# A linear attention followed by a two-layer perceptron on one core: rows of w, u and g spread by matmul, more transposes by DMA, and a new order

## The chip, the cores and the metric

The kernel runs on one core of a Trainium2 chip. The metric is the time on the device in microseconds (us) of one execution. The core has five engines that take their instructions each in its own order and wait for one another by semaphores: TensorE (PE in the profile; PEld is its loading of weights), VectorE (DVE), ScalarE (ACT), GpSimd (POOL) and SyncE (SP), which here only issues DMAs. ACT and POOL can issue DMAs too. All queues share 16 DMA engines.

## What is computed

Inputs r, k and v have 4 batches, 8 heads, 768 steps and 48 channels a head; w and u have one value for each head and channel. For each batch and head a 48 x 48 state is carried over the steps:

```
cur   = outer(u * k_t, v_t)
y_t   = r_t @ (state + cur)
state = w[:, None] * state + outer(k_t, v_t)
```

The heads are joined to rows x of 384 values (4 x 768 rows). Then each row goes through a LayerNorm and a perceptron with a residual:

```
xn  = (x - mean(x)) / sqrt(var(x) + 1e-6) * g
out = x + relu(xn @ w_ch1) @ w_ch2        # 384 -> 1536 -> 384
```

All inputs and the output are fp32.

## The kernel before, in words

The steps are cut into 24 chunks of 128 (chunk i is steps 128*(i % 6) onward of batch i // 6). In a chunk the recurrence is turned into matmuls: with Fr = w^t and Fk = w^(-t-1), scaled rows r*Fr and k*Fk make a score matrix, which is masked to the strictly lower part; the state of the chunks before enters by one more product, and the term with u is a factor per head and step (cc) times v. For each chunk there are these steps, with the names that the order uses:

- LK, LR, LV load k, r and v (192 KB each, in runs of 192 B). SK and SR scale k and r and write them as bf16 to sc. CV makes v bf16.
- TR transposes sc on PE, eight 128 x 128 blocks, and TC copies the result from PSUM to trs. From some chunk on TD does both at once, a DMA transpose from sc to trs.
- Q multiplies the two halves of trs. AT makes the scores on PE, and AM masks them into A (DVE).
- S makes on PE the factors cc (by uwI, which holds u*w) and the chunk's addition to the state; CC copies cc out. ZU and ZD form the next state Z with WLZ = w^128.
- VB forms Vb = v*cc. Y makes on PE the state's and the scores' part of the result, and X (DVE) adds Vb, writes a row tile x and sums it up.

For each of the 24 row tiles the perceptron then has: SQ (ACT, the sum of squares), XN (subtract the mean and multiply by g, to xn in bf16), LT and XT (three transposes on PE and a copy to xT) or LTD (one DMA transpose for a whole group), UP (PE, hp = w1 times xT, a PSUM tile of 512 columns), RL (ReLU to hT, on ACT or DVE), DN (PE, four of the twelve blocks of the second matmul at a time), RS (POOL, the inverse deviation), OT (DVE, o*rs + x) and STO (store). Tiles go in groups: 0 to 7 alone, 8 to 19 in pairs, 20 to 23 alone. UP,16g+m is part m of group g, of three for a group of one tile and six for a pair; DN,4i+d is part d of tile i. The last tile is split into two halves of columns (DA, DB, OA, OB, SA, SB).

Nothing schedules this at run time. The string PLAN lists every step with its index and its engine ("v" DVE, "s" ACT, "g" POOL; a DMA with "-" is issued by SP, with "s" by ACT; PE steps have "-" as well), and each engine takes its instructions in the order of that list. Each kind of buffer is a ring of a given number (8 for k and r, 10 for v, 6 for sc and trs, 3 for xn, 4 for xT, 4 for hT). DU steps are dummy matmuls of so many columns, put into PE's order where it would otherwise be idle.

Ahead of the first chunk, w is loaded spread over 128 partitions (WB, from ACT's queue). ACT takes its logarithm (LN) and makes Fr and Fk (FR, FK: exponentials scaled by the partition's number). w and u are also loaded turned, a channel to a partition (ROWS, four DMAs of single values, L186); from these POOL makes uwI (UW) and ACT makes WLZ (WL). g is loaded spread as well (GB, L181). The weights come by six DMAs issued by POOL (IW1 and IW2, 384 KB each, L256 and L259), of which part n of w_ch1 and part n of w_ch2 are tiles of their own. MP clears the padding of sc, MI and MM make the identity and the mask.

Lines that the prediction speaks of: TR L284, AT L320, AM L330, S L351 to L364, Y L393 and L401, X L408, SQ L415, XN L421 and L422, RS L428 and L431, LTD L435, TD L305, LT L443, UP L458, RL L474 (ACT) and L476 (DVE), DN L486, OT L542, copies L163 (ACT) and L165 (DVE, POOL), products L168, loads L262 (k), L265 (r), L268 (v).

Of the kernel before, what the change touches and what calls it, by code (L numbers as in the profile page):

```python
# [7 lines left out]
FP32 = mybir.dt.float32  # L8
# [9 lines left out]
WB,0,s LK,0,- MP,2,v MI,0,g MP,1,v TL,0,s LR,4,- MP,5,v MP,3,v LR,0,- MW,0,v MP,0,v ROWS,3,- LN,0,s ROWS,1,- FR,0,s LR,1,- FK,0,s ROWS,2,- SK,0,v  # L18
LK,2,- LK,1,- SR,0,v ROWS,0,- MZ,0,v LV,0,- DU,7984,- TR,0,- MP,4,v LR,2,- TC,0,s SR,4,g LV,1,- MM,0,g DU,2848,- AT,0,- LK,3,- Q,0,g AM,0,v LK,4,-
LR,6,- CV,0,s SK,1,v LR,3,- UW,0,g WL,0,s SR,1,v LV,2,- DU,4720,- S,0,- SK,2,v Y,0,- GB,0,- TR,1,- ZU,0,v CC,0,s VB,0,g CV,1,s LK,6,- SR,2,v  # L20
TC,1,s LR,5,- SK,3,v LK,5,- Q,1,v DU,2704,- TR,2,- X,0,v LV,3,- S,1,- TC,2,s SK,4,v AT,1,- LV,4,- AM,1,v CC,1,s DU,1056,- TR,4,- LR,7,- SR,3,g
VB,1,v TC,4,s DU,448,- Y,1,- AT,2,- LK,7,- IW1,0,g X,1,v CV,2,s DU,224,- TR,3,- LV,5,- SR,6,v Q,2,g ZU,1,v TC,3,s LV,6,- AM,2,v SK,6,g DU,1712,-
S,2,- SQ,1,s LR,9,- XN,0,v IW1,1,g DU,656,- Y,2,- LV,7,- Q,4,v SK,5,g LT,0,- AT,3,- SR,5,v XT,0,v CC,2,v AM,3,v DU,1104,- TR,6,- Q,3,g TC,6,s
ZU,2,v VB,2,g DU,1216,- AT,4,- XN,1,v LR,8,- DU,592,- TR,5,- CV,3,s IW1,2,g X,2,v UP,0,- IW2,0,g AM,4,v TC,5,s S,3,- RL,0,s LT,1,- CC,3,v ZU,3,v
AT,5,- VB,3,g XT,1,s XN,2,v Y,3,- Q,5,g UP,17,- LR,10,- CV,4,s X,3,v SQ,2,s UP,1,- XN,3,v RL,17,s S,4,- RL,1,v LT,3,- UP,16,- XT,3,s ZU,4,v
SQ,3,s LK,8,- Y,4,- CC,4,v SR,7,g AM,5,v LT,2,- RL,16,s S,5,- UP,48,- IW2,1,g XT,2,s UP,18,- CC,5,s RL,48,s IW2,2,g AT,6,- RL,18,v UP,34,- RS,2,g
VB,4,v Q,6,g UP,32,- RL,34,s LK,9,- DN,0,- RL,32,v SK,7,g UP,50,- X,4,v LK,10,- UP,49,- RS,3,g AM,6,v RL,50,s TR,7,- CV,5,g RL,49,s UP,2,- XN,4,v
SQ,4,s UP,33,- TC,7,v RL,2,s RS,4,g Y,5,- Q,7,v RL,33,s LT,4,- VB,5,g AT,7,- SQ,0,s XT,4,v LV,10,- DN,1,- RS,0,g X,5,v UP,65,- XN,5,v DN,2,-
LV,8,- CV,6,v SR,9,g UP,64,- OT,0,v LT,5,- LV,9,- Y,6,- RL,64,v S,6,- RS,1,g DN,4,- AM,7,v CC,6,s RL,65,s LK,14,- SR,8,g DN,5,- XT,5,s CV,7,s
# [33 lines left out]
def kernel(  # L63
# [526 lines left out]
```

## Time and profile before

| | us |
|---|---|
| median of 3 runs (lowest to highest) | 162.78 (160.44 to 163.22) |
| the profiled execution | 160.98 |
| its span, first to last instruction | 159.2 |
| PE busy | 143.0 (90%) |
| DVE busy | 132.3 (83%) |
| POOL busy | 88.3 (55%) |
| ACT busy | 69.4 (44%) |
| DMA, mean rate | 167 GB/s |

Busy time is the time in which an engine has some instruction under way. Matmuls overlap one another, so a busy PE isn't yet PE at its best rate; the dummy matmuls count as busy too. "DMA share" in a stretch is the sum of what packets took on the 16 DMA engines, divided by 16 times the stretch; packets overlap, so it can pass 1. In a group of instructions (line, engine, operation, output<-inputs, shape, count) the two numbers behind the bar are the busy time in us and the mean of one in ns; behind the next bar stands the idle time of the engine ahead of them and what ended it. In the timeline a bracket holds the idle time before an instruction and what released it.

### The profile page before, as it was taken

Reading aid. Unit: us, or ns where it says so; the run is one execution under the profiler, and the core shown is the slowest. Engines: PE = TensorE matmul, PEld = TensorE weight load, DVE = VectorE, ACT = ScalarE, POOL = GpSimd, SP = SyncE. Lnnn points to the kernel's source line nnn. Section 1 sums busy time; section 2 is a strip of 40 time slices with the busy share of each in tenths; the row PEclk is TensorE's granted clock in tenths of the full one; section 3 lists DMA queues with packets and bytes.
Section 4 is the critical chain, followed back from the end, with each engine's and each line's share of the span. In section 5 each row is a group of like instructions: output and inputs, shape, how many; then the busy total and the mean of one; then the engine's idle time right before and its main releaser. Section 6 shows DMA issues by size and latency. Waiting matters only on the chain.

```text
span 159.2 us, 4407 instructions
## 1 busy us (share of the span) xinstructions
PE 143.0 (90%) x1769; PEld 109.1 (69%) x1769; DVE 132.3 (83%) x265; ACT 69.4 (44%) x155; POOL 88.3 (55%) x119
## 2 busy tenths in 40 slices
PE   5896959499999989799999988997999999999991
PEld 2244737398877777677787757784787767888881
DVE  2457998696899999998889999999979999996132
ACT  3427644653821844646653644614184412700510
POOL 2332465899594665979769865559327420850100
PEclk9999999999999999999999999999999999999999
DMA  3899999999989959999999999895899772314212
GB/s 89 156 173 211 184 184 191 216 199 232 198 157 182 192 110 215 168 218 122 247 235 183 219 224 145 207 214 105 180 215 197 157 195 45 124 29 124 99 54 101
DMA packets 100356, 26.64 MB, mean 167 GB/s; under 512 B 95344, under 2 KB 99952, under 8 KB 100336
## 3 DMA queue, kind: packets, MB, share of 16 engines
q1 hardware_dynamic: 98560, 23.80, 75.0%
q0 software_dynamic: 1632, 2.36, 8.9%
q8 instruction: 14, 0.23, 0.6%
q10 hardware_dynamic: 144, 0.20, 0.5%
q14 instruction: 6, 0.05, 0.1%
HBM read 19.27 MB, written 4.72 MB: 151 GB/s over the span
## 4 chain that ended last, share of the span: by engine, by line
DVE 37%; PE 29%; SPq 10%; POOL 8%; issue 8%; DMA 6%; ACT 0%; DVEq 0%; POOLq 0%
PE hp L458 13%; PE o L486 12%; DVE A L330 8%; DVE xn L422 6%; DVE x L408 4%; SPq L265 4%; DVE Z L168 3%; DMA kf<-in_k_dram 3%; DVE ot L542 3%; DVE hT L476 3%; DVE ZS L377 3%; POOL sc L168 3%; DVE sc L168 3%; DMA trs<-sc 2%; SPq L262 2%
## 5 line engine op out<-in xcount | busy, mean ns | idle before, releaser
L458 PE MATMUL hp<-xT,w_sb 128*128 128x128 bf16 (+1 forms) x648 | 57.6, 238 | 0.6 <-DVE hT L476 0.6
L486 PE MATMUL o<-w_sb,hT 128*128 128x384 bf16 x276 | 53.3, 326 | 2.9 <-DVE ot L542 2.9
L458 PEld LDWEIGHTS <-w_sb 128*128 128x128 bf16 x648 | 48.7, 114 | 5.2 <-issue 0.7
L474 ACT ACTIVATE hT<-hp 128x512 bf16<-128x512 f32 x51 | 30.2, 596 | 44.9 <-PE hp L458 44.3
L486 PEld LDWEIGHTS <-hT 128*128 128x128 bf16 x276 | 25.2, 97 | 15.5 <-issue 3.4
L330 DVE TENSOR_TENSOR A<-at,mask 128x1024 bf16<-128x1024 f32 x24 | 29.1, 1215 | 1.8 <-PE at L320 1.8
L383 POOL TENSOR_TENSOR Vb<-vf,cc 128x384 f32<-128x384 f32 x14 | 12.3, 876 | 13.7 <-DVE cc L165 7.0
L422 DVE SCALAR_TENSOR_TENSOR xn<-x,mu,g_bc 128x384 bf16<-128x384 f32 x24 | 19.0, 792 | 0.8
L168 POOL TENSOR_TENSOR sc<-rf,Fr 128x384 bf16<-128x384 f32 x14 | 15.6, 1117 | 7.2 <-DMA rf<-in_r_dram 7.2
L542 DVE SCALAR_TENSOR_TENSOR ot<-o,rs,x 128x384 f32<-128x384 f32 x23 | 14.0, 610 | 5.8 <-PE o L486 5.7
L168 POOL TENSOR_TENSOR q<-trs 128x512 bf16<-128x512 bf16 x13 | 16.3, 1251 | 2.3 <-ACT trs L163 2.2
L428 POOL TENSOR_SCALAR rs<-sq 128x1 f32<-128x1 f32 (+1 forms) x18 | 3.9, 217 | 23.5 <-ACT sqj L415 22.5
L168 POOL TENSOR_TENSOR sc<-kf,Fk 128x384 bf16<-128x384 f32 x12 | 13.4, 1119 | 5.8 <-DMA kf<-in_k_dram 5.8
L476 DVE TENSOR_SCALAR hT<-hp 128x512 bf16<-128x512 f32 x21 | 14.3, 683 | 2.6 <-PE hp L458 2.6
L408 DVE SCALAR_TENSOR_TENSOR x<-y,Vb 128x384 f32<-128x384 f32 x24 | 13.2, 550 | 2.8 <-POOL Vb L383 2.1
L415 ACT ACTIVATE sqj<-x,sm 128x384 bf16<-128x384 f32 x24 | 14.7, 613 | 1.8 <-DVE cc L165 1.1
L227 PE MATMUL o<-warm 128*128 128x512 bf16 x45 | 13.3, 433 | 1.7 <-DVE u_p L194 1.7
L163 ACT COPY trs<-tr 128x1024 bf16<-128x1024 bf16 x8 | 8.1, 1011 | 12.5 <-PE tr L284 12.5
L168 DVE TENSOR_TENSOR sc<-kf,Fk 128x384 bf16<-128x384 f32 x12 | 9.0, 750 | 5.0 <-ACT Fk L235 4.5
L431 POOL TENSOR_TENSOR rs<-rs,expo 128x1 f32<-128x1 f32 (+1 forms) x18 | 12.0, 668 | 1.5
L320 PE MATMUL at<-trs 48*128 48x128 bf16 x192 | 9.6, 219 | 1.8 <-DVE A L330 1.7
L163 ACT CAST vv<-vf 128x384 bf16<-128x384 f32 x16 | 8.1, 513 | 4.5 <-DMA vf<-in_v_dram 4.5
(66 smaller groups left out, 169.8 us busy)
## 6 DMA issues: line engine op xcount, KB each, us to landing
kf<-in_k_dram SPq DMA_DIRECT2D x24, 192.0 KB, 4.3
rf<-in_r_dram SPq DMA_DIRECT2D x24, 192.0 KB, 4.4
vf<-in_v_dram SPq DMA_DIRECT2D x24, 192.0 KB, 4.2
out_dram<-ot SPq DMA_DIRECT2D x23, 192.0 KB, 2.3
w_sb<-in_moe_w_ch_dram POOLq DMA_DIRECT2D x6, 384.0 KB, 5.9
trs<-sc SPq DMA_TRANSPOSE x15, 3.6
w_bc<-in_w_dram ACTq DMA_DIRECT2D x1, 192.0 KB, 3.8
g_bc<-in_moe_g_ln_dram SPq DMA_DIRECT2D x1, 192.0 KB, 5.7
```

The lines of the kernel that those rows point to most:

```text
L163: nc.scalar.copy(out=out, in_=in_)
L168: engines[e].tensor_tensor(out=out, in0=in0, in1=in1, op=ALU.mult)
L227: nc.tensor.matmul(out=warm_ps[0][:], lhsT=warm[:, :P], rhs=warm[:], start=True, stop=True)
L330: nc.vector.tensor_tensor(out=AA(i)[:, a:b].rearrange("p e q t -> p (e q) t"), in0=psum["at", i][:, a:b].rearrange("p e q t -> p (e q) t") ...
L408: nc.vector.scalar_tensor_tensor(out=xx(i)[:], in0=psum["y", i][:, :C], scalar=1.0, in1=Vb(i)[:], op0=ALU.mult, op1=ALU.add, accum_out=sm[ ...
L415: nc.scalar.activation(out=sqj[:], in_=xx(i)[:], func=ACT.Square, bias=sm[i][:], scale=-float(C), accum_out=sq[g][:, j : j + 1])
L422: nc.vector.scalar_tensor_tensor(out=xn(g)[:, j], in0=xx(i)[:], scalar=mu[i][:], in1=g_bc[:], op0=ALU.subtract, op1=ALU.mult,)
L458: nc.tensor.matmul(out=t[:, a * gw : (a + 1) * gw], lhsT=w1_sb[n][:, kc, fb::FB], rhs=xT(g)[:, :size, kc, :], start=(kc == 0), stop=(kc == ...
L474: nc.scalar.activation(out=o, in_=s, func=ACT.Relu)
L476: nc.vector.tensor_relu(out=o, in_=s)
L486: nc.tensor.matmul(out=psum["o", i][:, :C], lhsT=hT(g)[:, fk, j * P : (j + 1) * P], rhs=w2_sb[d][:, a, :], start=(fk == 0), stop=(fk == FK ...
L542: nc.vector.scalar_tensor_tensor(out=ot(i)[:], in0=psum["o", i][:, :C], scalar=rs[g][:, j : j + 1], in1=xx(i)[:], op0=ALU.mult, op1=ALU.add,)
```

## The change

w, u and g are each loaded as a single row on one partition (WF by SP; UF and GF by ACT). LN works on that row. A matmul with a column of ones (WBM, one partition deep, fp32) spreads the row of logarithms to 128 partitions in PSUM, from where FR and FK read it. GBM spreads g in the same way, and GB is now DVE's copy out of PSUM. UWR (POOL) makes u*w on the row, and WT turns the rows of logarithms and of u*w into columns by eight matmuls with one column of ones each; UW (DVE, two copies) and WL (ACT) read these. The spread DMAs WB and GB and the four ROWS are gone, and so is a logarithm in WL. MO is a step of DVE with three small memsets.

XN may also be POOL's: there it is the mean, a subtraction to a new tile xc, and a product. MP may be POOL's.

DMA transposes of k and r begin with chunk 8 (before: 9), those of the LayerNorm rows with tile 8, group 8 (before: tile 16, group 12): 16 TD and 10 LTD instead of 15 and 6, 8 TR and 8 LT instead of 9 and 16. The list of steps is a new one throughout, with other engines for many steps. By count (before, after): XN on POOL 0, 6; SK on POOL 12, 16; SR on POOL 14, 11; CV on POOL 6, 11, on ACT 16, 7, on DVE 2, 6; VB on POOL 14, 15; ZD on POOL 6, 7; RL on DVE 21, 15; XT on ACT 12, 5, on DVE 4, 3; TC on ACT 8, 6, on DVE 1, 2; MP on POOL 0, 4. Q stays at 13 on POOL. Dummy columns: 25,264 before, 15,664 after.

```diff
 PLAN = """
-WB,0,s LK,0,- MP,2,v MI,0,g MP,1,v TL,0,s LR,4,- MP,5,v MP,3,v LR,0,- MW,0,v MP,0,v ROWS,3,- LN,0,s ROWS,1,- FR,0,s LR,1,- FK,0,s ROWS,2,- SK,0,v
-LK,2,- LK,1,- SR,0,v ROWS,0,- MZ,0,v LV,0,- DU,7984,- TR,0,- MP,4,v LR,2,- TC,0,s SR,4,g LV,1,- MM,0,g DU,2848,- AT,0,- LK,3,- Q,0,g AM,0,v LK,4,-
...
+MW,0,v UF,0,s LK,0,- MP,3,v MP,1,g MO,0,v GF,0,s WF,0,- LR,1,- TL,0,s LR,0,- LV,0,- LN,0,s UWR,0,g DU,2992,- WBM,0,- LR,4,- MP,2,g MI,0,g LK,1,-
+MP,0,g MP,4,g GBM,0,- MM,0,g FK,0,s LK,2,- FR,0,s SK,0,g WT,0,- SR,1,v LV,1,- SR,0,v MZ,0,v LR,2,- DU,432,- TR,0,- WL,0,s SK,1,g TC,0,v LV,3,-
+Q,0,v DU,2208,- TR,1,- LV,2,- GB,0,v CV,0,v TC,1,s DU,464,- AT,0,- CV,1,v LK,3,- SK,2,v UW,0,v Q,1,g AM,0,v DU,1632,- S,0,- LK,5,- CV,3,g SR,2,v
+LR,3,- DU,1120,- Y,0,- AT,1,- ZU,0,v TR,2,- CC,0,v LK,4,- AM,1,v VB,0,g S,1,- TC,2,s LR,5,- IW1,2,g X,0,v CV,2,g ZU,1,v DU,1968,- Y,1,- SQ,0,s
+LV,4,- Q,2,v AT,2,- IW1,1,g CC,1,v SR,3,v DU,272,- S,2,- VB,1,g SK,3,v AM,2,v CC,2,s DU,240,- TR,3,- TC,3,s X,1,v LK,6,- XN,0,v Q,3,g XN,1,v
+DU,3616,- LT,0,- AT,3,- XT,0,s ZU,2,v IW1,0,g AM,3,v DU,720,- UP,2,- SK,4,g LT,1,- Y,2,- RL,2,s MP,5,v XT,1,v SR,4,g S,3,- LR,6,- UP,18,- ZU,3,v
...
+DN,25,- CV,11,s X,9,v UP,112,- XN,9,v LR,14,- DN,26,- AM,10,v RL,112,s RS,7,g LTD,8,- UP,114,- SR,13,g S,10,- OT,6,v UP,113,- LK,14,- SK,11,v ZD,9,g AT,12,-
+SR,11,g RL,113,s DN,28,- TD,11,- SQ,9,s ZU,10,v SR,14,g DN,29,- SK,13,v RL,114,s AM,12,v Y,10,- SQ,8,s STO,3,- UP,129,- CC,10,s TD,13,- VB,10,g UP,133,- ZD,10,v
...
+RL,240,s UP,242,- X,23,v DN,84,- RL,242,s XN,23,v UP,256,- SQ,22,s LTD,17,- DN,85,- RL,256,v UP,257,- UP,258,- RL,257,s DN,86,- SQ,23,s UP,272,- RL,258,s RS,17,g OT,21,v
+UP,273,- RS,16,g STO,21,- DN,88,- RL,273,s DN,89,- RL,272,s DN,90,- UP,274,- OT,22,v DB,0,- RL,274,s STO,22,- DA,0,- DA,1,- STO,20,- DA,2,- DB,1,- OA,23,v DB,2,-
+SA,23,- OB,23,v SB,23,-
 """
...
-    w_bc = const.tile([P, C], FP32, name="w_bc")
+    w_row = const.tile([1, H, D], FP32, name="w_row")
+    u_row = const.tile([1, H, D], FP32, name="u_row")
+    g_row = const.tile([1, C], FP32, name="g_row")
+    ones = const.tile([1, P], FP32, name="ones")
+    ln_row = const.tile([1, H, DP], FP32, name="ln_row")
+    uw_row = const.tile([1, H, DP], FP32, name="uw_row")
...
-    def WB(i, e):
-        queues[e].dma_start(out=w_bc[:], in_=spread(w))
-
-    def GB(i, e):
-        queues[e].dma_start(out=g_bc[:], in_=spread(moe_g_ln))
...
+    def row(t):
+        return bass.AP(tensor=t.tensor, offset=t.offset, ap=[[C, 1], [1, C]])
+
+    def WF(i, e):
+        queues[e].dma_start(out=w_row[:].rearrange("p h d -> p (h d)"), in_=row(w))
...
     def LN(i, e):
-        nc.scalar.activation(out=ln_bc[:].rearrange("p h d -> p (h d)"), in_=w_bc[:], func=ACT.Ln)
+        nc.scalar.activation(out=ln_row[:, :, :D], in_=w_row[:], func=ACT.Ln)
+
+    def WBM(i, e):
+        t = psum["wb"] = ps.tile([P, 512], FP32, name="y")
+        nc.tensor.matmul(out=t[:, :C], lhsT=ones[:], rhs=ln_row[:, :, :D], start=True, stop=True)
+        psum["ln"] = t[:, :C].rearrange("p (h d) -> p h d", h=H)
...
+    def GB(i, e):
+        copy(e, g_bc[:], psum["gb"][:, 0].rearrange("p q t -> p (q t)")[:, :C])
+
+    def UWR(i, e):
+        times("g", uw_row[:, :, :D], u_row[:], w_row[:])
+
+    def WT(i, e):
+        t = psum["wt"] = ps.tile([P, 512], FP32, name="s")
+        first = True
+        for a, src in enumerate((ln_row, uw_row)):
+            flat = src[:].rearrange("p (q e) d -> p q (e d)", e=2)
+            for q in range(HP):
+                nc.tensor.matmul(
+                    out=t[:, a * HP + q : a * HP + q + 1], lhsT=flat[:, q, :], rhs=ones[:, :1],
+                    start=first, stop=True, skip_group_check=True,
+                )
+                first = False
...
     def XN(i, e):
         g, j, _ = group_of[i]
-        nc.vector.tensor_scalar(out=mu[i][:], in0=sm[i][:], scalar1=1.0 / C, scalar2=None, op0=ALU.mult)
-        nc.vector.scalar_tensor_tensor(
-            out=xn(g)[:, j], in0=xx(i)[:], scalar=mu[i][:], in1=g_bc[:], op0=ALU.subtract, op1=ALU.mult,
-        )
+        engines[e].tensor_scalar(out=mu[i][:], in0=sm[i][:], scalar1=1.0 / C, scalar2=None, op0=ALU.mult)
+        if e == "v":
+            nc.vector.scalar_tensor_tensor(
+                out=xn(g)[:, j], in0=xx(i)[:], scalar=mu[i][:], in1=g_bc[:], op0=ALU.subtract, op1=ALU.mult,
+            )
+        else:
+            nc.gpsimd.tensor_scalar(out=xc[:], in0=xx(i)[:], scalar1=mu[i][:], scalar2=None, op0=ALU.subtract)
+            times(e, xn(g)[:, j], xc[:], g_bc[:])
```

## The prediction

> **What bounds the kernel now.** I read the busy lines of the page first, then stretches of the span, then the timeline of the front, then the groups and the chain.
>
> ```profile
> PE 143.0 (90%) x1769; PEld 109.1 (69%) x1769; DVE 132.3 (83%) x265; ACT 69.4 (44%) x155; POOL 88.3 (55%) x119
> ...
> DVE 37%; PE 29%; SPq 10%; POOL 8%; issue 8%; DMA 6%; ACT 0%; DVEq 0%; POOLq 0%
> ```
>
> No engine alone is the limit: the chain that ended last runs 37% on DVE and 29% on PE. By stages (us; then busy time and instructions of PE, PEld, DVE, ACT, POOL; clock, DMA share, GB/s):
>
> ```profile
> 0.00:27.00 27.00, 21.22 (x211) 12.08 (x212) 18.51 (x42) 12.29 (x21) 10.56 (x22) 1.00 0.92 169
> 27.00:40.00 13.00, 10.72 (x196) 9.66 (x193) 9.77 (x22) 7.04 (x17) 12.10 (x16) 1.00 1.17 214
> 40.00:130.00 90.00, 85.18 (x1064) 67.18 (x1063) 85.26 (x166) 42.40 (x101) 59.30 (x71) 1.00 0.96 187
> 130.00:145.00 15.00, 15.00 (x183) 11.34 (x182) 14.64 (x31) 4.69 (x12) 5.58 (x11) 1.00 0.30 72
> ```
>
> For 27 us PE does little that counts: the 25,264 columns of dummy matmuls (at 512 columns in 0.216 us, the spacing once it runs fast, 10.7 us) lie here. From 40 to 130 us PE and DVE are both 95% busy, and from 130 us on PE sets the pace. So time can be won by starting the perceptron sooner, by taking work from PE, and, between 40 and 130, by taking work from DVE too. The front in the timeline (start, duration):
>
> ```profile
> 15.80 1.18 SPq L181 DMA_DIRECT2D g_bc<-in_moe_g_ln_dram  x1
> ...
> 22.95 0.14 DVE L421 TENSOR_SCALAR mu<-sm 128x1 f32<-128x1 f32 x1
> 23.12 0.72 DVE L422 SCALAR_TENSOR_TENSOR xn<-x,mu,g_bc 128x384 bf16<-128x384 f32 x1
> ...
> 27.22 0.83 PE L458 MATMUL hp<-xT,w_sb 128*128 128x128 bf16 x12
> ...
> 30.93 0.40 PE L320 MATMUL at<-trs 48*128 48x128 bf16 x8 [1.74 <-DVE A L330]
> ```
>
> The first row is normalized at 23.1, the first UP runs at 27.2, and PE then idles 1.7 us before 30.9. The first DN runs at 38.6 (in the chain); its weight load was the last but two of POOL's six, issued at 29.9, and these take 5.9 us to land.
>
> **The front, step by step.** Removed: two 128-fold spreads (192 KB each; g_bc takes 5.7 us to land, issued amid loads that take 4.3) and four ROWS transfers, which hold SP for 0.70+0.44+0.58+1.12 = 2.8 us, with GB's 1.18 4.0 us. Up to 40 us the DMA share is 0.92 to 1.17 and SP issues almost without a pause, so the loads of k, r and v behind these come some 4 us sooner.
>
> Against that the path to Fk grows. WF stands second on SP, as an rf load did at 1.24; I let it land at 4.6, which is when w_bc was there (bounds: 2.5 us after issue, as w_p took, gives 3.7; behind kf, 5.0). LN on one row has as many elements per lane, 0.5 us. WBM is an fp32 matmul, which the trace lacks: from below the bf16 row of 384 columns, 0.33; from above four times it, 1.3, since both operands are twice as wide; I take 0.9, nearer the upper end because PE is slow here (below). Fk 0.6 ends at 6.6, Fr at 7.2; before they ended at 6.3 and 5.8. Then SR,1 and SR,0 on DVE, 2 x 0.6: TR,0 at 8.4 instead of 8.2. GBM and WT (nine more fp32 matmuls, bounds 0.5 and 3 us) run beside Fk, Fr and the products.
>
> Next DVE sets the order. Between TR,0 (0.6) and the first XN it does, by the rows: TC 0.68, two Q 0.42, GB about 0.5, two CV 0.76, SK 2 x 0.55, SR 2 x 0.55, UW 2 x 0.15, three AM 1.22, two ZU 0.55, two CC 0.16, two X 0.63: 12.4 us. XN,0 starts at 8.4+0.6+12.4 = 21.4 and XN,1 follows at once; before they ran at 23.1 and 26.7. With LT 0.34 and XT 0.48 the first UP can run at about 23.5. Its weights are IW1,2, behind VB,0 on POOL, about 16 + 5.9 = 22. **Gain at the first UP: 3.7 us.** The IW2 issues follow about 9 us of POOL work after VB,0 (three Vb 0.88, Q 1.25, two CV 0.67, SK and SR 1.1, three issues 0.8), so they go at 26 to 29 instead of 30 to 35, and the first DN can run near 32. That is a gain of 3.7 to 6; **I take 4.5** and keep 2 to 6.
>
> A dummy matmul of 512 columns follows the one before it after 0.43 us up to 5.5 us, and after 0.22 us later, although the page's clock reads 1.00 throughout. The new plan has 2992 columns of them first instead of 7984 and then waits for WBM; slow transposes and AT up to about 12 us would cost up to 1 us of the 4.5. The Trainium skill (TensorE: Matmul & The Clock Gate, Part 1) says that the array starts at half clock and is released after about 3.4 us of sustained work; the trace agrees, 0.43 against 0.22. By that rule alone the front would gain 3.5 rather than 4.5.
>
> **The rest, engine by engine.** PE: LT falls from 16 tiles to 8 and TR from 9 chunks to 8, 24 + 8 transposes. At the 0.056 us spacing that twelve 128-column matmuls in 0.67 us show, that is 1.8 us, at the durations of the groups (0.34 and 0.61) 3.3 us. Nothing hides it where PE is the pace; Most of it lies where DVE is as busy as PE and gains nothing from it, so I count less than the lower end, **1.3**.
>
> DVE: 6 XN go to POOL (6 x 0.93), 6 RL to ACT (6 x 0.68), 4 SK, one VB, one ZD and one XT leave (3.0+0.7+0.95+0.35), 4 CV, 3 SR, one TC and GB come (3.0+2.0+0.7+0.5): 132.3 falls by about 8.5. ACT loses 9 CV, 7 XT, 2 TC and gains 6 RL: 69 to 63, and it has slack.
>
> POOL: 6 XN, each mu 0.19, a subtraction that no row shows (between a CAST 0.50 and a product 1.12; I take 0.8) and a product 1.1; 5 CV 0.67, 4 SK less 3 SR 1.1, a VB 0.9, a ZD 1.1, the memsets 1.4: 88 to 108 us. It is done by about 140, so it is over 80% busy where it was 65%.
>
> ```profile
> L422 DVE SCALAR_TENSOR_TENSOR xn<-x,mu,g_bc 128x384 bf16<-128x384 f32 x24 | 19.0, 792 | 0.8
> L168 POOL TENSOR_TENSOR sc<-kf,Fk 128x384 bf16<-128x384 f32 x12 | 13.4, 1119 | 5.8 <-DMA kf<-in_k_dram 5.8
> ```
>
> xn has a median of 0.62 us and a longest of 1.34, and every long one lies beside a POOL instruction. Over xn, sc, Vb, Z and q the excess over the shortest is 11.8 us in 73 instructions. After, 64 of them remain, beside a POOL busier by 108/88: 64 x 0.16 x 1.22 = 12.6, **a loss of 0.9**. The Trainium skill (GPSIMD Engine Reference, 8. Key points) says that GpSimd shares its SBUF interfaces with VectorE and contends with instructions of two SBUF inputs; the trace agrees, since hT, which reads PSUM alone, stays between 0.67 and 0.69.
>
> DMA and SP: one TD and four LTD of two tiles more. They are taken at 3.6 and 2.5 us to landing and hold SP 1.24 and 1.2 each, 6 us, against the 4.0 us that went from the front. Each LTD waits on SP for both XN of its group (the four such waits before summed to 10.3 us, 3.7 at most), and behind it stand the loads and the TD of the next chunks: behind LTD,8 these are LK,14, TD,11, STO,3 and TD,13, for which Q, AT and AM of chunks 11 and 13 wait. Loads run several chunks ahead, so I price this at 0.5, bounds 0 and 10. No queue but SP's sees it.
>
> Tail: between Y,23 and the first UP of tile 23 stood ten groups of 0.66 us, now seven, 4.6 us. They hide X 0.63, XN 0.93 and LTD 2.3 to 2.5; 0.5 is spare. With the longest landing, 5.4, it would cost 2.5. I count 0.4.
>
> **Sum**, against the profiled execution's own 160.98 (span 159.2): -4.5 - 1.3 + 0.9 + 0.5 + 0.4 = -4.0, 157.0. The median of the three runs shown is 162.78, 1.8 above that execution; some of it may recur, so I say 157.4.
>
> **The rivals.**
> The DVE relief counts in full. If DVE is what holds PE in the middle, its 8.5 us give 4 more: 153. For it: 37% of the chain; against it: PE is as busy there.
>
> DMA becomes the bound in the middle. In the trace the 21 transposes are 18,432 packets of 256 B that take 30.1 us of all 16 engines, 1.4 each; five more at a share already 0.96 give back 5 to 7 us: 162. For it: shares over 1 between 70 and 100 us. Against it: in 40 to 130 the chain meets DMA in single places only, the largest 3.9 us for one trs.
>
> SP held by slow POOL rows, the case that ends slower. XN on POOL takes 2.1 instead of 0.9 us behind a longer POOL queue, LTD holds SP for it, and the TD behind it comes late, whose chunk PE then lacks. The place is tiles 8 to 17. It decides once an LTD holds SP more than about 3 us, the lead of the transposes (3.6 to landing); at 2 us over for each of five groups it costs 10: 160.98 - 4.5 - 1.3 + 10 = 165.
>
> The front brings nothing, as the fp32 path to Fk or cold matmuls delay the first chunk by as much as the loads gain: 161.
>
> **Chances.** Forecast 0.49, full DVE relief 0.14, DMA 0.14, SP held 0.14, no front 0.09. The range reaches from 152 (front 6, DVE relief) to 163.5, which leaves out the SP case and little else. Runs of this kernel differ by 1.7%, so 2% is about what can be told: faster 0.62, within 2% 0.23, slower 0.15.
>
> **What would show it.** First UP near 23.5, first DN near 32, no idle on PE of over 1 us between them; DVE near 124 and POOL near 108 us; trs and xT landing in 3 to 4 us; SP waits at the LTD line under 3 us each. I am wrong if the first UP is after 26, if PE idles over 8 us between 40 and 130 (4.8 now), or if the waits at LTD are long and AT or Q follow them late.

## The result and the profile after

The changed kernel is slower. Its median is 167.87 us (167.34 to 168.75, 4 runs) against 161.66 us (160.44 to 163.22) for the kernel before on the same chip: a ratio of 1.042, with a 95% interval of 1.029 to 1.054. The ratio compares the means without runs in the chip's slower state; one of the four before, at 163.22, was in it. The profiled execution took 167.34 us, its span is 165.3 (before: 160.98 and 159.2). The forecast of 157.4 was wrong in sign, and the range of 152 to 163.5 missed.

First the page of the changed kernel, its busy line and its chain:

```profile
PE 146.9 (89%) x1733; PEld 112.4 (68%) x1736; DVE 131.4 (80%) x247; ACT 63.8 (39%) x143; POOL 112.3 (68%) x148
...
DVE 33%; PE 31%; POOL 17%; DMA 9%; issue 4%; SPq 4%; ACT 0%; DVEq 0%; POOLq 0%
```

POOL's share of the chain went from 8% to 17%, and DVE, which should have lost some 8.5 us of work, lost 0.9. The same stretches as before, with the same columns (length; busy time and instructions of PE, PEld, DVE, ACT, POOL; clock, DMA share, GB/s):

```profile
0.00:27.00 27.00, 22.99 (x178) 14.59 (x181) 18.07 (x37) 8.22 (x14) 14.79 (x28) 1.00 1.00 185
27.00:40.00 13.00, 10.97 (x179) 10.16 (x180) 10.11 (x18) 7.11 (x16) 7.25 (x11) 0.87 1.09 206
40.00:130.00 90.00, 81.44 (x999) 62.98 (x996) 80.54 (x149) 35.57 (x85) 77.06 (x91) 1.00 0.89 164
130.00:145.00 15.00, 14.70 (x160) 10.89 (x159) 12.62 (x26) 5.96 (x15) 8.24 (x13) 1.00 0.99 196
```

Three things differ from before. The clock of PE is 0.87 from 27 to 40 us, where it was 1.00. From 40 to 130 PE idles 8.6 us instead of 4.8 and DVE 9.5 instead of 4.7, while POOL is busy 77.1 of 90 us instead of 59.3. And PE runs 999 matmuls there instead of 1064.

A count of busy time hides how much is done, so I counted work: each matmul that belongs to the result, at the spacing with which its kind follows itself in the traces (162 ns for DN's 384 columns, 109 and 56 for UP's, 55 for a transpose, 43, 42 and 25 for the parts of Y and S; for AT I took 40). Dummies and the fp32 matmuls are left out. In us of such work per stretch:

| | to 40 | 40 to 70 | 70 to 100 | 100 to 130 | 130 to 150 | rest | sum |
|---|---|---|---|---|---|---|---|
| before | 16.8 | 27.5 | 27.2 | 26.8 | 19.5 | 5.6 | 123.4 |
| after | 15.0 | 25.5 | 24.4 | 26.7 | 18.2 | 11.9 | 121.6 |

So the changed kernel is 1.8 us behind at 40 us, loses 2.0 and 2.8 in the next two stretches, nothing from 100 to 130 and 1.3 up to 150: 8.0 in all (the columns are rounded), of which 1.8 need not be done, for the transposes that went to the DMA. That leaves 6.2, and the span is 6.1 longer.

**The front.** PE's timeline of the changed kernel (start, duration, line, operation), then the same place before:

```profile
3.88 1.64 PE L236 MATMUL y<-ln_row,ones 1*128 1x384 f32 x2
5.32 1.48 PE L247 MATMUL at<-g_row,ones 1*128 1x384 f32 x2
6.59 1.70 PE L263 MATMUL s<-ones,ln_row 1*128 1x1 f32 x8
8.16 1.84 PE L263 MATMUL s<-ones,uw_row 1*128 1x1 f32 x8
9.93 0.54 PE L229 MATMUL o<-warm 128*128 128x432 bf16 x1
10.27 1.06 PE L312 MATMUL tr<-ident,sc 128*128 128x128 bf16 x8
11.12 1.91 PE L227 MATMUL o<-warm 128*128 128x512 bf16 x4
```

```profile
8.23 0.62 PE L284 MATMUL tr<-ident,sc 128*128 128x128 bf16 x8 [1.00 <-DVE sc L168]
8.69 1.24 PE L227 MATMUL o<-warm 128*128 128x512 bf16 x5
```

WBM is two instructions of 0.6 to 0.8 us from start to start, GBM is two more, and the eight matmuls of WT are 16 instructions that together hold PE from 6.6 to 10.0. TR,0 runs 2 us later than before because it stands behind them (in e5, below, where it doesn't, its data are there at 8.5), and takes 1.06 instead of 0.62. The first four dummies behind TR,0 follow one another after 0.43 us where before they did so after 0.22: PE is still at half speed at 13 us. AT,0 runs at 14.3. The first Y comes at 16.3, 3.3 us later than before (a Y is timed here, and below, by the start of its last part, the eight products with the scores). The dummies have a share in that: TR,1 could have run at 12.1, when its input had been there for 2 us and the copy of TR,0 had freed its buffer, but it ran behind the last of them, at 13.0, and AT,0 behind 0.5 us more of them. No run took them out.

Then DVE and POOL of the changed kernel from 23 us on, in the timeline:

```profile
23.40 1.44 DVE L451 SCALAR_TENSOR_TENSOR xn<-x,mu,g_bc 128x384 bf16<-128x384 f32 x1
...
24.94 3.98 DVE L451 SCALAR_TENSOR_TENSOR xn<-x,mu,g_bc 128x384 bf16<-128x384 f32 x1
...
25.19 1.01 POOL L170 TENSOR_TENSOR sc<-kf,Fk 128x384 bf16<-128x384 f32 x1
...
25.82 0.83 PE L490 MATMUL hp<-xT,w_sb 128*128 128x128 bf16 x12
26.16 1.00 POOL L170 TENSOR_TENSOR sc<-rf,Fr 128x384 bf16<-128x384 f32 x1
...
27.11 0.82 POOL L411 TENSOR_TENSOR Vb<-vf,cc 128x384 f32<-128x384 f32 x1
27.88 0.61 POOL L287 DMA_DIRECT2D w_sb<-in_moe_w_ch_dram  x1
28.51 1.25 POOL L170 TENSOR_TENSOR sc<-kf,Fk 128x384 bf16<-128x384 f32 x1
...
28.97 0.50 PE L475 MATMUL tr<-ident,xn 128*128 128x128 bf16 x3 [2.32 <-DVE xn L451]
```

XN,1, a row that takes 0.62 us alone, lasts 3.98 us: it begins when POOL is about to start a run of instructions without a pause (SK,4, SR,4, VB,2, an IW2 issue, SK,5), and ends 0.4 us into the last. Behind it on DVE wait the next state and scores (ZU,2, AM,3) and, through LT,1, the second and all later UPs. The first UP ran at 25.8, 1.4 us sooner than before; PE then had next to nothing to do:

```profile
24.00:28.00 4.00, 1.59 (x24) 1.27 (x25) 3.96 (x3) 1.08 (x2) 3.98 (x6) 1.00 1.25 219
28.00:32.00 4.00, 2.97 (x36) 2.67 (x37) 3.89 (x8) 0.00 (x0) 2.30 (x3) 0.57 1.23 229
```

PE is busy 1.6 us of four, and in the next four its clock is 0.57. The first DN runs at 37.3 (before 38.4), so of the gain that the forecast put at 4.5 us one is left, and chunk 2 (Y,2 at 29.6, before 23.1) is 6.5 us behind.

**From 36 to 54 us.** The same columns, first before, then after:

```profile
36.00:54.00 18.00, 18.00 (x277) 15.21 (x276) 15.91 (x32) 7.91 (x19) 12.23 (x18) 1.00 0.97 189
```

```profile
36.00:54.00 18.00, 16.66 (x229) 13.00 (x227) 13.95 (x23) 8.95 (x20) 16.73 (x24) 1.00 0.51 91
```

POOL is busy 93% of the time, PE and DVE less than before, and the DMA share falls to 0.51. More is said below with the chain.

### The profile page after: what moved, and what is told of

It is laid out like the page before. It is cut to its first block, busy times and chain, and to the rows that moved or that the text cites. A ratio compares the mean times of both kernels' runs of the same rounds, so it can differ in the third digit from the quotient of the medians.

```text
span 165.3 us, 4343 instructions
## 1 busy us (share of the span) xinstructions
PE 146.9 (89%) x1733; PEld 112.4 (68%) x1736; DVE 131.4 (80%) x247; ACT 63.8 (39%) x143; POOL 112.3 (68%) x148
## 3 DMA queue, kind: packets, MB, share of 16 engines
q1 hardware_dynamic: 101842, 24.65, 77.1%
## 4 chain that ended last, share of the span: by engine, by line
DVE 33%; PE 31%; POOL 17%; DMA 9%; issue 4%; SPq 4%; ACT 0%; DVEq 0%; POOLq 0%
PE hp L490 10%; DVE A L358 8%; PE o L518 8%; DVE xn L451 5%; DVE sc L170 5%; DMA kf<-in_k_dram 4%; POOL xc L455 4%; POOL xn L170 3%; DVE ot L574 3%; DMA out_dram<-ot 3%; PE o L227 2%; DVE x L436 2%; POOL rs L463 2%; POOL q L170 2%; PE s L263 2%
## 5 line engine op out<-in xcount | busy, mean ns | idle before, releaser
L490 PEld LDWEIGHTS <-w_sb 128*128 128x128 bf16 x648 | 49.9, 114 | 6.5 <-issue 2.5
L506 ACT ACTIVATE hT<-hp 128x512 bf16<-128x512 f32 x57 | 33.4, 596 | 54.2 <-PE hp L490 53.8
L411 POOL TENSOR_TENSOR Vb<-vf,cc 128x384 f32<-128x384 f32 x15 | 12.9, 860 | 11.9 <-ACT cc L165 8.9
L170 POOL TENSOR_TENSOR sc<-kf,Fk 128x384 bf16<-128x384 f32 x16 | 17.0, 1063 | 4.6 <-DMA kf<-in_k_dram 4.5
L170 DVE TENSOR_TENSOR sc<-rf,Fr 128x384 bf16<-128x384 f32 x13 | 9.8, 764 | 4.8 <-ACT Fr L243 4.2
L170 POOL TENSOR_TENSOR sc<-rf,Fr 128x384 bf16<-128x384 f32 x11 | 12.3, 1116 | 1.9 <-DMA rf<-in_r_dram 1.8
L508 DVE TENSOR_SCALAR hT<-hp 128x512 bf16<-128x512 f32 x15 | 10.3, 685 | 3.4 <-PE hp L490 3.4
L170 POOL TENSOR_TENSOR Z<-ZS,WLZ 128x384 bf16<-128x384 f32 x7 | 8.1, 1152 | 5.8 <-DVE mu L449 3.5
L165 ACT COPY trs<-tr 128x1024 bf16<-128x1024 bf16 x6 | 6.1, 1012 | 12.1 <-PE tr L312 12.1
L460 POOL TENSOR_SCALAR rs<-sq 128x1 f32<-128x1 f32 (+1 forms) x18 | 5.2, 292 | 5.9 <-ACT sqj L443 4.6
L348 PEld LDWEIGHTS <-trs 48*128 48x128 bf16 x192 | 5.8, 95 | 5.0 <-issue 3.0
```

What stands on the lines that cost most here:

```text
L170: engines[e].tensor_tensor(out=out, in0=in0, in1=in1, op=ALU.mult)
L348: nc.tensor.matmul(out=t[:, par, q, :], lhsT=trs(i)[p0 : p0 + D, 1, q, :], rhs=trs(i)[p0 : p0 + D, 0, q, :], start=True, stop=True,)
L411: engines[e].tensor_tensor(out=Vb(i)[:].rearrange("p (h d) -> p h d", h=H), in0=vf(i)[:], in1=cc(i)[:].unsqueeze(2).to_broadcast([P, H, D] ...
L490: nc.tensor.matmul(out=t[:, a * gw : (a + 1) * gw], lhsT=w1_sb[n][:, kc, fb::FB], rhs=xT(g)[:, :size, kc, :], start=(kc == 0), stop=(kc == ...
L506: nc.scalar.activation(out=o, in_=s, func=ACT.Relu)
```

## The experiments

All times are medians beside runs of the kernel before on the same chip, which had medians of 161.4 to 161.9. "Order before" and "order after" are the two lists of steps.

| | edit | us | ratio to before (95%) |
|---|---|---|---|
| after | | 167.87 | 1.042 (1.029 to 1.054) |
| e1 | order before, rows | 163.90 | 1.015 (1.009 to 1.021) |
| e2 | order before, transposes by DMA | 172.78 | 1.066 (1.057 to 1.074) |
| e3 | order before, six XN on POOL | 169.19 | 1.048 (1.041 to 1.055) |
| e4 | after, all XN on DVE | 168.56 | 1.046 (1.038 to 1.054) |
| e5 | after, WT behind TR,0 | 170.25 | 1.055 (1.049 to 1.061) |
| e6 | after, SK,4 and SR,4 on DVE | 166.32 | 1.030 (1.024 to 1.036) |
| e7 | after, four loads ahead of STO,0 | 168.42 | 1.041 (1.036 to 1.047) |
| e8 | after, stores issued by ACT | 169.56 | 1.047 (1.040 to 1.054) |
| e9 | after, transposes back on PE | 172.46 | 1.067 (1.061 to 1.074) |
| e10 | e9 and all XN on DVE | 172.25 | 1.067 (1.060 to 1.073) |
| e11 | front of after, then order before | 167.76 | 1.040 (1.036 to 1.044) |
| e12 | e9, transposes spaced | 174.05 | 1.076 (1.070 to 1.081) |
| e13 | e10, transposes spaced | 171.04 | 1.058 (1.053 to 1.064) |
| e14 | after, XN,1 later | 165.91 | 1.025 (1.020 to 1.030) |
| e15 | e14 and e6 | 166.64 | 1.029 (1.023 to 1.035) |
| e16 | e14, two XN and three CV off POOL | 163.95 | 1.020 (1.013 to 1.027) |
| e17 | e11 without its stall | 166.31 | 1.032 (1.022 to 1.041) |
| e18 | e16, two more XN off POOL | 163.92 | 1.021 (1.013 to 1.028) |

### Each part alone, in the order before (e1, e2, e3)

```diff
 # e1: the new functions, the order before
-WB,0,s  ROWS,0,- ROWS,1,- ROWS,2,- ROWS,3,-  GB,0,-
+WF,0,s UF,0,s GF,0,s MO,0,v
 LN,0,s
+DU,2992,- WBM,0,-
-DU,7984,-
+DU,3000,-
 TR,0,-
+GBM,0,- GB,0,v UWR,0,g WT,0,-
 # e2: chunk 8, and tiles 8 to 15 in their four pairs
-TR,8,- TC,8,s
+TD,8,-
-LT,8,- XT,8,s LT,9,- XT,9,s        (and so to tile 15)
+LTD,8,-                            (behind the second XN of the pair)
 # e3
-XN,3,v XN,4,v XN,8,v XN,10,v XN,16,v XN,18,v
+XN,3,g XN,4,g XN,8,g XN,10,g XN,16,g XN,18,g
```

> The kernel before with the single rows of w, u and g and their fp32 matmuls, in the order of before; WT and GBM stand behind TR,0 on PE and the dummy columns are split so that WBM does not wait for them. Theory 'order' (the parts are harmless, the new order of the steps loses the time): 1 to 4 us faster than before, as the loads behind the spread transfers land some 4 us sooner, though the order of before can use only part of that. Theory 'front' (the fp32 matmuls delay the first chunk by as much as the loads gain): 0 to 2 us slower. Theories 'POOL' and 'SP' say nothing of it.

> The kernel before with TD for chunk 8 and LTD for the groups 8 to 11 (tiles 8 to 15) in place of TR, TC, LT and XT, each LTD right behind the later XN of its pair, all else in the order of before. Theory 'SP' (each LTD holds SP for its XN, and the loads and TD behind it come late): 4 to 8 us slower than before. Theories 'POOL' and 'order': within 1.5 us of before, as 32 transposes of PE and 9 copies go and 5 transfers come.

> The kernel before with XN of tiles 3, 4, 8, 10, 16 and 18 on POOL as three instructions, nothing else changed. Theory 'POOL' (the six rows take 2.5 us each on POOL, hold DVE off the shared SBUF side and stand in the chain): 3 to 7 us slower than before. Theories 'SP' and 'order': within 1.5 us, since DVE gets 5.6 us back.

Each part by itself costs: 2.0, 10.9 and 7.3 us against the 161.89 of the kernel before, run beside them. The rows delay the first Y from 13.0 to 17.1 and the first UP to 31.5, and the following stretches are as good as before (27.6, 27.6 and 27.1 us of work from 40 to 130). In e2 what PE waits for from 40 to 150 us reads (engine, line, what it waited for: us, times, longest):

```profile
PE hp L451 <- DMA xT<-xn: 7.2, 4, 4.3
PE at L313 <- DMA trs<-sc: 3.1, 1, 3.1
```

A transpose by DMA lands some 3 us after its issue, and in an order made for a 0.3 us transpose on PE the UPs stand too close behind it. In e3 POOL's share of the chain is 22% (before 8%), and PE waits for POOL's Q and xn, 2.5 and 1.5 us. So neither the DMA nor POOL hides its work by itself; a part can only be free if the order leaves room for it.

### Is it the SP queue (e7, e8)?

At STO,0 SP waits for the result of tile 0 (OT,0), and the timeline shows a hole of more than 6 us, then another at TD,9:

```profile
31.13 5.76 SPq L290 DMA_DIRECT2D kf<-in_k_dram  x2
43.23 0.37 SPq L581 DMA_DIRECT2D out_dram<-ot  x1
43.66 0.43 SPq L296 DMA_DIRECT2D vf<-in_v_dram  x1
50.50 1.34 SPq L333 DMA_TRANSPOSE trs<-sc  x1
```

```diff
 # e7
+LV,8,- LR,10,- LV,7,- LK,12,-
 STO,0,-
 # e8: 23 stores
-STO,0,-
+STO,0,s
```

> The changed kernel with LV,8, LR,10, LV,7 and LK,12 ahead of STO,0 and TD,9 in SP's order. In the changed kernel SP issues nothing from 36.9 to 43.2 us (STO,0 waits) and from 44.1 to 50.5 (TD,9 waits), with v of chunk 7 behind both. Theory 'SP': S,7 and Y,7 come some 4 us sooner and the time falls by 2 to 4 us. Theories 'front' and 'POOL': less than 1 us.

> The changed kernel with the 23 STO issued by ACT instead of SP, so that no load and no transpose stands behind a store's wait; ACT has 40% busy time. Theory 'SP': 2 to 5 us faster than the changed kernel. Theories 'front' and 'POOL': within 1.5 us either way, or slower where ReLUs on ACT then stand behind a store's wait.

Neither helps: 168.4 and 169.6. In e7 the DMA share from 36 to 54 us rises from 0.51 to 0.71, as the loads go sooner, but POOL is busy 16.73 us in it as before, PE 16.41, and Y,7 comes at 67.5 instead of 67.2. e8 says less, since ACT then has a wait of its own (one hT stands 3.0 us behind a store). SP waits for others; PE's matmuls hardly wait for what SP issues: in the changed kernel once between 30 and 150 us, 0.8 us for an xT. SP's own longest waits are for DVE, at TD, at STO and at LTD:

```profile
SPq L333 <- DVE sc L170: 11.9, 8, 6.3
SPq L581 <- DVE ot L574: 11.2, 3, 6.3
SPq L467 <- DVE xn L451: 7.9, 7, 2.8
```

### The front (e5, e6, e14, e15)

```diff
 # e5
-FR,0,s SK,0,g WT,0,- SR,1,v ... TR,0,-
+FR,0,s SK,0,g SR,1,v ... TR,0,- WT,0,-
 # e6
-SK,4,g ... SR,4,g
+SK,4,v ... SR,4,v
 # e14
-XN,0,v Q,3,g XN,1,v ... UP,2,- SK,4,g LT,1,- Y,2,- RL,2,s MP,5,v XT,1,v SR,4,g S,3,- ... ZU,3,v ... UP,1,- ... RL,1,v
+XN,0,v Q,3,g ... UP,2,- SK,4,g Y,2,- RL,2,s MP,5,v S,3,- ZU,3,v XN,1,v UP,1,- LT,1,- RL,1,v XT,1,v SR,4,g
 # e15: e14 with SK,4 and SR,4 as in e6
```

> The changed kernel with WT (eight fp32 matmuls of one column, 3.5 us of PE ahead of TR,0) behind TR,0. Theory 'front' (a late first chunk is not made up for later): TR,0 moves from 10.3 to about 8.5 us and the time falls by 1 to 2 us. Theories 'SP' and 'POOL': the gain is lost at the next waits, within 1 us of the changed kernel.

> The changed kernel with SK,4 and SR,4 on DVE instead of POOL. In the changed kernel they run on POOL back to back while XN,1 on DVE takes 3.98 us instead of 0.62. Theory 'front': XN,1 falls under 1.5 us, LT,1 and UP,18 run some 2 us sooner, and the time falls by 1 to 3 us. Theory 'SP': less than 1 us, since the loads and TD,9 behind STO,0 stay where they are; theory 'POOL' 1 to 3 us as well, by two products less on POOL.

> The changed kernel with XN,1 (its VectorE row took 3.98 us) and LT,1, XT,1 moved behind S,3 and ZU,3, so that ZU,2, AM,3 and with them Y,2 and S,3 come ahead of it; UP,1 ahead of UP,18. If the late products of the front (Y,2 at 29.6) and the clock of 0.52 to 0.63 at 28 to 32 us are what the front costs, Y,2 ends by 27.5, the clock stays at 1.0, and the time falls by 1.5 to 3: 165 to 166.5. If only the order further on counts: 167 to 169.

> e14 with SK,4 and SR,4 on VectorE as in e6. If both cure the same loss, no more than the better of the two (165 to 166.5); if they add, 163.5 to 165.

e5: TR,0 does run at 8.48, where the prediction had it, but WT then stands ahead of TR,1 and AT,0, which runs at 16.1 instead of 14.3, and the later Y come 1.6 to 1.9 us later, up to the last (153.1 against 151.2). PE is the bound of the front, with fp32 matmuls and dummies at half speed; moving one of them only moves the wait.

e6: with two products fewer on POOL beside it, XN,1 takes 2.06 instead of 3.98 us; the clock stays at 1.00, the first DN runs at 35.7 instead of 37.3, and the time falls by 1.6.

e14: the work of DVE that chunks 2 and 3 need comes ahead of XN,1, which then takes 0.79. Y,2 comes at 26.9 (29.6), the last Y at 149.8 (151.2). The stretches of the front in e14:

```profile
24.00:28.00 4.00, 2.60 (x47) 2.07 (x48) 3.18 (x5) 1.08 (x2) 3.98 (x5) 1.00 1.25 218
28.00:32.00 4.00, 3.07 (x50) 2.75 (x51) 3.71 (x10) 1.02 (x2) 2.55 (x4) 1.00 1.23 226
```

PE no longer starves, its clock stays at 1.00 (the mean is 1.000 in every run of e14 and of e6, and 0.979 to 0.990 in those of the changed kernel), and the time is 165.91, 2.0 under the changed kernel. e15 is no better, nor is its run with a mean clock of 1.000 (166.64): both cure the same loss. That loss is therefore about 2 us: the long row, what waits behind it, and the clock.

### Transposes and order (e9 to e13, e17)

```diff
 # e9
-TD,8,-
+TR,8,- TC,8,s
-LTD,8,-
+LT,8,- XT,8,s LT,9,- XT,9,s        (groups 9 to 11 likewise)
 # e10: e9, and XN,3 4 8 10 16 18 on DVE
 # e12, e13: e9 and e10, but the first LT of a pair stands sooner, two PE steps or more ahead of the second
 # e11: the order after up to the first UP, then all steps left, in the order before
 # e17: e11, but XN,1 where the order before has it, Y,2 and VB,2 right behind UP,0
```

> The changed kernel with chunk 8 and tiles 8 to 15 turned by TensorE again (TR,8 with its copy, LT and XT in the place of each LTD), all else as changed. If the transposes by DMA cost in the changed order what they cost in the order before (172.8 against 161.9 there, some 10 us), this gives 158 to 161. If the new order is what loses the 4 to 5 us between 40 and 130, and was searched with these transposes in it, it gives 167 to 170: the wide transposes cost nothing where their waits are laid out for them, and 32 more matmuls on TensorE cost 1 to 2 us.

> As e9 (changed kernel, chunk 8 and tiles 8 to 15 turned by TensorE), but the transposes of the two tiles of a group stand at least two steps apart on TensorE, where e9 had them back to back and the second waited 0.73 us for the copy of the first, five times. If the 4.6 us of e9 over the changed kernel are these waits and the 1.8 us of transposes, this gives 168 to 170. If the transposes by DMA are what costs in the changed order, 162 to 166.

> The changed order with the rows, with all transposes of e9 on TensorE and all LayerNorm rows on VectorE: against the order before with the same rows (163.9), only the order differs. Order theory: 167 to 171, and TensorE idles 8 us or more between 40 and 130. If the moved work (transposes by DMA, rows on GpSimd) is the cause instead, this gives 162 to 165 and TensorE idles under 6 us there.

> As e10 (the changed order, old work but for the rows) with the same spacing: against the order before with the same rows (163.9), only the order differs. Order theory: 167 to 170. If the order is no worse than the one before, 162 to 165, and e10's 172.3 was the spacing alone.

> The changed kernel's steps up to the first UP, then the remaining steps in the order before (transposes of chunk 8 and of tiles 8 to 15 by TensorE, rows of the LayerNorm on VectorE, SR,4 on VectorE, UP,0 and IW2,0 first). Order theory: the stretch from 40 to 130 loses nothing against before, and the time is 160 to 163, the front's 1.4 us given or taken. If the front is what costs (chunk products 3 to 6 us later than before, carried to the end), it gives 164 to 167.

> e11 with the stall of its front taken away: XN,1 stays where the order before has it (behind AT,4), Y,2 and VB,2 come right behind the first UP. The rest in the order before. If the front with rows can be had without its stall, and the order before loses nothing further on, this gives 160 to 163 and may beat the kernel before. If the front's fp32 matmuls and later products cost what they cost in e1, 163.5 to 166.

With the transposes back on PE the order after takes 172.46 and 174.05, 4.6 and 6.2 us more than the changed kernel. So in this order the DMA transposes are no loss, where in the order before they cost 10.9: the order has room for their 3 us. How large the gain is stays unsure, since I put the steps back by hand. The second LT of a pair waits for the copy of the first, four times in e9 and three in e10, as in this place of e10's PE timeline:

```profile
73.12 0.33 PE L468 MATMUL tr<-ident,xn 128*128 128x128 bf16 x3
74.01 0.33 PE L468 MATMUL tr<-ident,xn 128*128 128x128 bf16 x3 [0.57 <-ACT xT L158]
```

In e13, where they are spaced, these waits are gone. e13 against e1 has the same work, and differs in the order alone: 171.04 against 163.90. By the count of work e13 is 1.1 us behind e1 at 40 us (13.3 against 14.4) and loses 4.0 from 70 to 100 us (23.6 against 27.6). In its front XN,1 takes 3.96 us, LT,1 waits 2.3 us for it, and the clock falls for longer than in the changed kernel:

```profile
28.00:32.00 4.00, 2.81 (x34) 2.50 (x35) 3.97 (x7) 0.00 (x0) 2.46 (x4) 0.56 1.23 228
32.00:36.00 4.00, 4.00 (x51) 4.00 (x50) 2.19 (x7) 1.91 (x3) 0.00 (x0) 0.58 1.11 217
```

From 83.1 to 86.5 us it is at half again, behind a wait of AT for a trs (1.8 us). So the order after, with the steps as I put them back, is worse than the order before for the old work; but the 7.1 us hold the collision of XN,1 too, worth some 2 us in e14, and what a better placing would save is open.

e11 and e17 keep the new front and go on in the order before. From 40 us on e11 is as good as the kernel before (28.6, 27.4 and 26.7 us of work in the three stretches), but at 40 us it has done 11.1 us of work, before 16.8, and the first DN runs at 44.2. In the front of the changed kernel the first UP is early, but the chunks are late; the order before wants the chunks. PE's clock is part of this loss: from 28.3 to 38.5 us it is at half while PE is busy 8.1 of these 10.2 us, and the mean clock is 0.959 to 0.969 in all five runs of e11 (0.977 to 0.979 in e17). Both are slower than e1 (163.90), so the new front is no gain ahead of the order before.

### POOL from 36 us on (e4, e16, e18)

The chain of e14, in order of time (start, us, what):

```profile
35.61 1.28 POOL xc L448
...
36.96 1.01 POOL xn L163
...
41.09 1.12 POOL q L163
42.21 1.28 POOL sc L163
...
43.91 1.26 POOL xc L448
...
45.25 1.00 POOL xn L163
46.25 0.97 POOL sc L163
47.22 1.56 POOL vv L160 x2
48.78 0.98 POOL sc L163
49.77 0.93 SPq L326
```

From 35.6 to 49.8 it is POOL alone, and nothing that it waits for: XN,3 and XN,4 (each mu 0.23, xc 1.27, the product 1.0), and behind them three RS (2.7 us) and the Q, scalings and copies of chunks 5 to 10. In the changed kernel itself POOL is the chain from 37.5 to 44.1 us, and then PE and DVE are. The low DMA share there, 0.51, isn't shown to follow from POOL: SP's two long waits, 6.3 us each, are for OT,0 and for a scaling on DVE.

```diff
 # e4: the order after, XN,3 4 8 10 16 18 on DVE
 # e16: e14 with
-XN,3,g XN,4,g CV,5,g CV,6,g CV,8,g
+XN,3,v XN,4,v CV,5,s CV,6,s CV,8,s
 # e18: e16 with
-XN,8,g XN,10,g
+XN,8,v XN,10,v
```

> The changed kernel with all 24 XN on DVE, at the places of the list where they stand, nothing else changed. Theory 'POOL': 3 to 6 us faster than the changed kernel, 162 to 165 us. Theory 'SP' or 'order': 0 to 2 us from the changed kernel, 166 to 169 us.

> e14 (165.9) with XN,3 and XN,4 on VectorE and the copies CV,5, CV,6 and CV,8 on ScalarE instead of GpSimd. In e14's chain GpSimd runs without a break from 35.6 to 49.7 us, with two rows (2.5 us each), the copies (0.8 each) and chunks 9 and 10's scalings behind them, and TD,9 waits for the last. If GpSimd is the bound of that stretch, taking some 7 us from it gives 163 to 164.5. If VectorE is as late there, as in e4 (168.6 against 167.9), 165.5 to 167.5.

> e16 (163.95) with XN,8 and XN,10 on VectorE as well. In e16's chain the rows of these two on GpSimd (67.9 to 70.6 and 79.7 to 82.4) stand with what is queued behind them (scalings, a Z, two Q, two VB) between 66 and 91 us. If GpSimd is the bound of that stretch too, 5 us less on it give 161.5 to 163.2, level with the kernel before. If VectorE, which then has the rows, is as late there, 163.5 to 165.5.

e16 takes 163.95 us, 2.0 less than e14 (163.55 to 165.08 against 165.35 to 166.19), 3.9 less than the changed kernel. The stretch, first in e14 and then in e16:

```profile
36.00:54.00 18.00, 16.64 (x223) 12.80 (x222) 14.28 (x26) 7.50 (x16) 16.82 (x23) 1.00 0.60 113
```

```profile
36.00:54.00 18.00, 17.17 (x242) 13.43 (x240) 15.86 (x31) 8.88 (x19) 10.33 (x16) 1.00 0.71 139
```

POOL falls from 16.8 to 10.3 us, DVE takes the rows (14.3 to 15.9 us), and the chain of e16 is a weight load up to 40 us (the last IW2, issued by POOL at 34.1), then PE itself up to 48.3, and DVE from there to 56.5:

```profile
34.09 5.91 DMA w_sb<-in_moe_w_ch_dram
...
41.60 0.70 PE hp L483 x12
42.30 0.65 PE o L511 x4
42.96 0.45 PE tr L305 x8
43.40 1.30 PE o L511 x8
```

e4 took the same two rows and four more from POOL and gained nothing in the end, 168.56. Its Y show why: Y,7 comes 1.5 us sooner than in the changed kernel and Y,15 1.9 sooner (99.8 against 101.7), but Y,21 no sooner (141.8 against 141.9). From 100 to 130 us, where the rows of tiles 16 and 18 are, it does 24.5 us of work against 26.7, and PE waits 3.1 us for DVE against 1.4. Rows on POOL cost in the stretch where POOL is the bound and pay where DVE is late; a test that moves all six at once sees the difference only. e18 fits that: two more rows taken from POOL, and 163.92, the same as e16. Between 70 and 100 us POOL is not what holds PE alone. The profiles put the size of e16's gain in doubt, not its sign: from 40 to 70 us PE does 24.8 us of work in e14 and 27.0 in e16, but 25.6 in e18, which has the same edits there and was profiled in its slowest run (164.94).

e16 and e18 are 2% slower than the kernel before (1.3 to 2.8% by the intervals); no version here beats it.

## Why the prediction was wrong, step by step

**Front, 4.5 us of gain.** This is where it failed first. "TR,0 at 8.4" with GBM and WT "beside Fk, Fr and the products": they stood ahead of TR,0 in PE's order, took 4.6 us (my upper bound was 3), and TR,0 ran at 10.27. The 2.0 us went on: XN,0 at 23.4 instead of 21.4, the first UP at 25.8 instead of 23.5. That they went on one for one is partly luck: DVE took 12.1 us from TR,0's end to XN,0 where the sum had 12.4, but 0.8 of them it idled, waiting for AT,0. The slow matmuls cost PE more than the 1 us that I allowed: TR,0 and TR,1 took 1.06 instead of 0.6 and the dummies between them and AT,0 twice their time, 2.0 us together. Then "XN,1 follows at once": it did, at 24.9, and lasted 3.98. The IW2 issues, put at 26 to 29, came at 27.9, 29.7 and 36.4, the last behind a VB that POOL waited 5.3 us for. The first DN, put near 32, ran at 37.3. e14 and e6 show this second step to be worth about 2 us, and e5 that the first isn't mended by moving WT behind TR,0. At 40 us PE had done 1.8 us less of the work than before, where the forecast had 4.5 us more.

**The contention term, +0.9.** The sum was mis-sized, and the place was missed. Over the same instructions (xn, sc, Vb, Z and q on DVE) the excess over the shortest of each kind was 12.1 us in 73 before (I had written 11.8) and is 16.7 in 64 after, where I had 12.6. XN,1 alone has 3.4 of it. Without that one the estimate by averages would have been right to 1 us, which is the trap: an average prices a collision as if it were spread, and this one stood on the path that set the front. I cited only that the two engines contend. The Trainium skill (SBUF — State Buffer, SBUF: two separate sides) says more: the shared port pair is an exclusive lock, whoever comes first holds it for a whole instruction, and the other blocks fully. The trace fits that and goes beyond it, since the row lasted until 0.4 us into the fifth POOL instruction beside it; that it lost the lock to each of them is my inference.

**POOL at 108 us, "over 80% busy", at no price.** POOL came out at 112.3, with xc at 1.39 us on average where I took 0.8. I priced its load for DVE and for SP, but gave it no term as the bound of a stretch. Stretch by stretch the profile after shows it: 93% from 36 to 54 us. e16 shows that term to be 2.0 us.

**DVE, 132.3 less 8.5.** It is 131.4. The relief was eaten by the contention (+4.6 over before, by the sums above); the three memsets of MO, 1.1 us, were not in the sum; the rest of the difference I did not trace. So the relief that the forecast refused to count, and that a rival at 153 counted in full, wasn't there.

**PE, 1.3.** The work that went is 1.8 us by count, as worked out, and shows only as that: between 40 and 100 us PE lost 4.8 elsewhere. The condition that I gave for being wrong, over 8 us of idle PE from 40 to 130, was met with 8.6.

**DMA and SP, 0.5, and the rivals.** xT lands 2.9 us after its issue and trs 3.6, and the longest wait at LTD is 2.8, all as said. The rival that SP is held by slow POOL rows, with 165, came nearest in time, and half of its cause was right: slow rows on POOL delay what is queued behind. But it was wrong on the way: another order on SP gains nothing (e7, e8), and the part that e16 wins back is POOL's own queue. "DMA bound" falls with a share of 0.89 in that stretch, less than before. "The front brings nothing" was right as far as it went, but it had no price for what the front took from the middle. The tail's 0.4 did not occur: from 150 us on PE waits for nothing.

**What I did not weigh at all** was the order. The DMA transposes cost 10.9 us in the order before, and in the order after it cost 4.6 to 6.2 to take them back by hand; and the order after is worse than the order before for the old work as I put it back (e13 against e1, the collision of XN,1 included). The parts can't be priced one by one and added up: e1, e2 and e3 sum to 20 us, the whole costs 6.

**What is settled and what is open.** Of the 6.2 us, 2.0 are the collision of XN,1 with its wake (e14), 2.0 the load of POOL from 36 to 54 us (e16). 2.6 remain in e16 and 2.1 in e18, each against the kernel before beside it. In the order before the rows cost 2.0 (e1), which would account for most of them, but that this is so in the order after was not tried: no run had this order with the old front. In e16 PE still does 1.6 us less from 70 to 100 us than before, which e18 did not cure.

## What to carry to other kernels

When work is moved to an engine with slack over the whole run, look at its busy share in the stretch where the work lands, with what is queued behind it: here POOL, 55% busy before on average and 68% after, was 93% busy for 18 us, and taking work from it there gave back 2.0 us. Price a collision between two engines where it happens, not by its average, and see which instruction waits behind it. And put every instruction of a new step into the order of its engine, its small matmuls too: eight matmuls of one column each cost 3.3 us ahead of the first transpose.

## What was not expected of the hardware

- **Small fp32 matmuls did not bring PE up to speed.** In the changed kernel PE has instructions without a pause from 1.2 to 13 us, but from 3.9 to 9.9 they are fp32 on one partition. Dummies are 0.427 us apart up to 12.8 us and transposes 107 ns up to 13.6, and at 15.1 they are at 216 ns. Before, with dummies alone, full speed came at 5.6. The page's clock reads 1.00 in these stretches, so here it is the spacing that tells. In e1 PE was at full speed at 8.8 us (transposes 56 ns apart), ran GBM and WT from 9.0 to 11.5, and though it did not pause its clock was 0.50 from 12.2 to 15.6, with dummies 0.42 us apart. The Trainium skill (TensorE: Matmul & The Clock Gate, Part 1) has full speed after about 3.4 us of sustained work. Before, it took 3.9 us from the first dummy, and in e1 3.4 from the first behind WBM; in the changed kernel PE was still slow at 14.6, 4.7 us behind the last fp32 matmul. That these are the cause was not tried by itself.
- **The clock fell after 4 us of little work**: 1.6 us busy of four, then 0.57 (after), and not with 2.6 of four (e14), nor before, where 1.9 of four between 28 and 32 us left it at 1.00. In the traces it falls to 0.50 for 3.4 us at a time, or for two or three times that (6.8 us in e13, 10.2 in e11). Many other runs of the kernel before have a mean clock of 0.989, as one such fall would give, where the profiled one has 1.000.
- **A DVE row beside POOL can last through several POOL instructions in a row**: 3.98 us beside five of them, 2.06 beside fewer (e6), 0.79 (e14), while rows of 0.62 beside a POOL product also occur throughout.
- **The price of small operations**: an fp32 matmul of 384 columns is two instructions of 0.64 us from start to start at that clock, one of a single column two of 0.21. On POOL a subtraction of one value per partition over 128x384 in fp32 takes 1.26 us at least, longer than the product of two such tiles with 1.0.
